# Attention and a feed-forward block in one kernel: other costs and delays in its planner, and the order that follows from them

## The chip, the cores and the metric

The kernel runs on one core of a Trainium2 chip. The metric is the device time of one execution in microseconds (us). The profile shows one execution: its engines are TensorE (PE, with its weight loads as PEld), VectorE (DVE), ScalarE (ACT), GpSimd (POOL) and SyncE (SP), which here only issues DMAs.

## The reference

Two parts follow each other. The first is attention in which a query sees only the keys of its own hash bucket; the second is a feed-forward block with an exact GELU.

```python
# q, k, v: (4, 8, 768, 64) float32; proj: (64, 6)
q_bits = (einsum('bhsd,dk->bhsk', q, proj) > 0)      # 6 bits
k_bits = (einsum('bhsd,dk->bhsk', k, proj) > 0)
mask = bucket(q_bits) == bucket(k_bits)               # (.., 768, 768)
scores = where(mask, q @ k.T / sqrt(64), -1e9)
attn = softmax(scores)                                # over the keys
x = (attn @ v) -> (3072 tokens, 512)                  # heads side by side
h = x @ w_in                                          # (3072, 2048)
g = 0.5 * h * (1 + erf(h / sqrt(2)))
out = g @ w_out                                       # (3072, 512)
```

## The kernel before, in words

All products with float32 accuracy are made of float16 matmuls: each operand is split into a high and a low half, and three products are summed (`TERMS`). Part of the first batch is done with float32 matmuls instead (`WHOLE`), which need more of PE and less of DVE.

The work is cut into *units*: 128 queries of one head against all 768 keys, 4 x 8 x 6 = 192 of them. A unit (`unit`, line 794) is a chain: four score matmuls on PE into one of two PSUM banks (ring `s`, lines 816 and 817), the row maximum on DVE (line 820), two one-column DVE instructions (guard, line 824, and shift, line 829), the exponential on ACT (line 832), which frees the bank, the norm on DVE (line 842), the split into high and low half (line 386 or 383 on any of three engines, line 848 on DVE), and a DMA that transposes the result for the product with the values (line 946). In the float32 units matmuls against a diagonal do the transpose (line 889) and line 937 the product.

Before a head's units can run, the head is prepared (`head`, line 525): load, maximum on DVE (line 537), a tiny "total" matmul on PE (line 494, in `head_scale`), a few one-column DVE instructions (lines 497 to 512), the split (line 386 or 383, 568 or 406), copies between partitions, the hash projection on PE (line 602), its sign on ACT and the mask rows. Each batch has a scale of its values (`v_scale`, maxima in line 748), and the weights are decoded, scaled and split in eight batches (`weight_pair`, lines 652 to 706). When a batch's scale and all weights are there, `hidden_scales` (lines 1087 to 1093) makes the scales of the feed-forward block on DVE.

The feed-forward block goes over 24 groups (12 chunks of 256 tokens, two halves of the 2048 hidden columns): hidden matmuls on PE (line 1120), an ACT copy out of PSUM (line 1130), GELU on ACT (line 1154), the split of its result (line 386 or 383, then 1168), the output matmuls (line 1192) and, after the second half, the drain on DVE (line 1213) and the store. Four PSUM banks (ring `hp`) serve all matmuls but the scores.

There are five passes over the heads: 256 queries of the first batch, its other 512, then one pass for each of the other batches.

The order of all instructions is made while the kernel is being built. Each piece of work is a `Step` with an engine (or several possible ones), a cost in us, a key, the steps that it needs and, for some, a ring whose slot it takes. `Plan.order` (line 110) runs the steps through a list scheduler on an imagined clock: whenever an engine is free, it takes, among the steps that are ready for it, the one with the smallest key plus its engine's offset. A step counts as ready for an engine a *hop* after the step that it needs has ended; a ring's slot is free when the last step that frees it has ended. Most rings give out their slots in program order; `hp` and `sign` to whoever comes first. The steps are then emitted in the order of their imagined starts, and on the chip each engine works through its own queue in that order, waiting on semaphores. Only the order is taken from the imagined clock, no time.

The keys are sums of a unit's running number `t` (0 to 191) and parameters of the table `PAR`: a head's key is `t` less its lead, its load subtracts `HQ` further, its maximum and total add `NS`; `VS0` is the key of the first batch's values and `SU` that of the set-up. The lead is `H0` to `H7` for the eight heads of the first pass, `G0` to `G7` for heads prepared anew in the second, and 6 + `HL` for the other batches. The feed-forward matmuls have keys from 1000 on, so PE takes them only when nothing of the attention is ready.

Of the kernel before, what the change touches and what calls it, by code (L numbers as in the profile page):

```python
# [19 lines left out]
P = 128  # L20
TC = 256
# [11 lines left out]
PAR = dict(  # L33
    SU=-208.01, NM_DVE=-120.92, NM_ACT=-21.45, NM_Pool=27.77, NM_SP=-123.06, NL_DVE=-286.91, NL_Pool=-152.59,
    NK_DVE=18.44, NK_ACT=149.22, NK_Pool=104.15, Z=-57.22, VS0=79.32, H0=-16.78, HL=-145.51, VS=19.55, G2=135.91,
    HQ=25.26, VQ=-257.12, in0=-297.08, out0=-226.11, in1=75.15, out1=-23.55, in2=208.31, out2=27.03, in3=-2.86,
    out3=-110.46, H1=295.79, H2=49.71, H3=-73.91, H4=30.82, H5=-111.35, H6=-305.61, H7=137.32, MEV=-105.25,
    MGE=-38.66, MSP=154.66, V0=61.1, QK0=151.51, QK1=139.57, QK2=162.2, MX0=-370.06, MX1=-267.83, MX2=36.74,
    EX0=32.1, EX1=300.62, EX2=464.34, NR0=126.59, NR1=149.21, NR2=345.77, HI0=-109.88, HI1=151.95, HI2=-108.38,
    LO0=-8.61, LO1=-97.74, LO2=-73.8, PV0=-123.13, PV1=19.87, PV2=-46.85, TR0=-116.16, TR1=246.71, TR2=162.28,  # L40
    V1=-192.5, V2=-1.2, Sin0=-172.88, Sin1=26.3, Sin2=-153.88, Sin3=140.04, Sout0=115.77, Sout1=-66.23,
    Sout2=146.63, Sout3=-97.45, Lin=-116.07, Pin=86.29, Qin=-266.79, Cin=76.33, Min=-479.07, Lout=304.56,
    Pout=-4.44, Qout=263.25, Cout=-138.23, Mout=364.95, G0=75.6, G1=-54.28, G3=101.75, G4=20.47, G5=15.54, G6=91.81,
    G7=-87.11, DUP0=339.38, DUP1=-11.03, DUP2=-81.43, LOW0=-236.86, LOW1=-108.93, LOW2=-52.33, PRJ0=3.84,
    PRJ1=29.31, PRJ2=211.23, MSK0=-134.81, MSK1=214.61, MSK2=42.29, DI_ACT=-147.41, DI_DVE=235.9, DI_Pool=21.15,
    WS_ACT=-362.67, WS_DVE=125.31, WS_Pool=315.49, WH_ACT=115.97, WH_DVE=-41.99, WH_Pool=-275.73, WL_ACT=74.46,
    WL_DVE=-184.87, WL_Pool=1.02, VH_ACT=5.16, VH_DVE=89.96, VH_Pool=-119.57, RND_ACT=-68.59, RND_DVE=20.61,
    RND_Pool=43.78, HI_ACT=54.52, HI_DVE=95.22, HI_Pool=-253.58, DG_ACT=203.58, DG_DVE=68.05, DG_Pool=-664.35,
    EV_ACT=-157.8, EV_DVE=400.19, EV_Pool=-118.56, GH_ACT=204.98, GH_DVE=104.62, GH_Pool=-464.69, NS0=-62.77,
    NS1=-38.83, NS2=-129.58,  # L50
)
# [19 lines left out]
class Plan:  # L71
# [38 lines left out]
    def order(self):  # L110
# [13 lines left out]
        events = []  # L124
# [16 lines left out]
        for t in set(free_at.values()):  # L141
            heapq.heappush(events, (t, -1, None))
        count = 0
        while events:
# [4 lines left out]
            for e in batch:  # L149
                if e is None:  # L150
                    continue
                for hold in e.frees:
                    hold["left"] -= 1
                    if not hold["left"]:
                        self.rings[hold["holder"].takes].append(hold["holder"].slot)
                for u in users.get(e, ()):
                    left[u] -= 1
                    for w in u.ways:
                        hop = self.SAME.get(w, 0.05) if w == e.engine else self.HOP[e.engine] + 0.12 * (w == "Pool")
                        at[u, w] = max(at.get((u, w), 0.0), now + hop)  # L160
                        heapq.heappush(events, (at[u, w], -1, None))
                    if not left[u]:
                        enlist(u)
            for engine, pool in ready.items():
# [18 lines left out]
                s = best  # L183
# [51 lines left out]
def tile_bucket_attention_moe(  # L235
# [252 lines left out]
    def head_scale(top, w, key, needs, n):  # L488
# [27 lines left out]
        pm = add("PE", 0.06 + 0.08 * n, total, key, needs, takes="hp")  # L516
        e = add("DVE", 0.12, exponent, key, [pm])
        free(pm, [e])
        e = add("DVE", 0.07, inverse, key, [e])
        if n > 1:  # L520
            e = add("DVE", 0.07, back, key, [e])
        return add("DVE", 0.07, scale, key, [e])

    def head(b, h, i, key, clear, cl):
# [19 lines left out]
        def add_move(dst, src, rd, rs):  # L544
            box = []

            def move():
# [6 lines left out]
            on = {  # L554
                "DVE": (0.27, PAR["NM_DVE"]), "ACT": (0.75, PAR["NM_ACT"]), "Pool": (0.9, PAR["NM_Pool"]),
                "SP": (0.45, PAR["NM_SP"]),
# [4 lines left out]
        def add_low(dst, rd, rs):  # L561
# [12 lines left out]

            on = {"DVE": (0.94, PAR["NL_DVE"]), "Pool": (2.8, PAR["NL_Pool"])}
            box.append(add(on, 0, low, key + PAR[f"LOW{cl}"], [hi], port=True))
# [32 lines left out]

        pp = add("PE", 0.45, project, key + PAR[f"PRJ{cl}"], [space, *set16], takes="hp")  # L610
        sg = add("ACT", 0.1 + 0.833e-3 * HS + 0.186, sign, key + PAR[f"PRJ{cl}"], [pp])
# [3 lines left out]
        for half in range(2):  # L615
            for k, dst in enumerate((0, 1)):
                box = []

                def mask(half=half, k=k, dst=dst, box=box):
# [181 lines left out]
    def unit(t, i, qs, cl, whole, made, place, back):  # L801
# [78 lines left out]
    def whole_turn(ex, nr, r, place, cl, t):  # L880
# [22 lines left out]
        for n, (k0, k1) in enumerate(((0, KT // 2), (KT // 2, KT))):  # L903
            step = []
            step.append(
                add("PE", 0.23 * (k1 - k0), lambda k0=k0, k1=k1, step=step: product(k0, k1, step), t + PAR[f"LO{cl}"], [dg], takes="hp")
            )
# [14 lines left out]
    def values(b, pr, ch, whole, vhl, turns, holds, key):  # L922
# [31 lines left out]
        for n, kt in enumerate(range(0, KT, 2)):  # L954
            kts = range(kt, min(kt + 2, KT))
            parts.append(
                add(
                    "PE", (0.96 if whole else 0.70) * nt / TC, lambda kts=kts: product(kts), key, [vh, vl, xt[b, ch], *turns, *parts],
                    takes=None if n else "hp",
                )  # L960
            )
# [119 lines left out]
    def hidden_scales(b):  # L1081
# [20 lines left out]
    for n, (b, ch, g) in enumerate(groups):  # L1102
# [8 lines left out]
        for fp in range(GF // 2):  # L1111
# [73 lines left out]
        for us in blocks:  # L1185
            for f in range(GF):
# [88 lines left out]
```

## Time and profile before

| | us |
|---|---|
| median of 3 runs | 929.64 (928.78 to 930.78) |
| the profiled execution | 928.35 |
| its span, first to last instruction | 926.4 |
| PE busy in the span | 857.1 |
| DVE busy | 734.4 |
| ACT busy | 607.8 |
| POOL busy | 347.1 |
| mean granted clock of PE | 0.983 |

A row of the profile names the line, the engine and the operation, what it writes and reads, how often it ran, its busy time and mean duration, and the idle time of the engine just before it with what ended that. A timeline row begins with its start and its length in us; a number in brackets at its end is the idle time of the engine before it. The granted clock of PE is 1.00 at full speed. Matmuls are pipelined: a row's length is longer than the distance to the next one.

### The profile page before, as it was taken

How to read it: one execution, taken by the hardware profiler on the slowest of the kernel's cores; microseconds unless marked ns; L12 is line 12 of the kernel's file. 1: busy time of each engine (PE TensorE's matmuls, PEld its weight loads, DVE VectorE, ACT ScalarE, POOL GpSimd, SP SyncE). 2: the span in 40 equal slices, each digit the busy share in tenths (PEclk: the TensorE clock that was granted, in tenths of full speed). 3: DMA queues.
4: the chain of work that ended last, by engine and by line, in shares of the span. 5: the costliest groups of instructions: out<-in, count | busy, mean ns of one | idle time of the engine just before them, and what ended most of it. 6: DMA issues, size and time to landing. Idle time of an engine off the chain costs nothing.

```text
span 926.4 us, 18281 instructions
## 1 busy us (share of the span) xinstructions
PE 857.1 (93%) x6857; PEld 576.7 (62%) x6857; DVE 734.4 (79%) x1734; ACT 607.8 (66%) x990; POOL 347.1 (37%) x323
## 2 busy tenths in 40 slices
PE   1578899996999999999999999999999999999998
PEld 0355667764575765666666666656666757575763
DVE  6888999999989999999999999899889961212122
ACT  4577799698877878757877777777865742222221
POOL 3444457285654354642335542454540400000000
PEclk9988999997999999999999999999999999999999
DMA  7653554538778788977686979788785760000000
GB/s 229 188 158 110 158 169 120 150 82 174 149 132 173 144 160 184 190 139 158 121 164 149 188 151 187 125 157 152 140 130 117 139 120 16 17 7 23 1 23 23
DMA packets 301848, 118.53 MB, mean 128 GB/s; under 512 B 241664, under 2 KB 290240, under 8 KB 301760
## 3 DMA queue, kind: packets, MB, share of 16 engines
q1 hardware_dynamic: 301680, 117.38, 58.9%
q8 instruction: 53, 0.87, 0.4%
q14 instruction: 35, 0.29, 0.1%
q10 hardware_dynamic: 80, 0.00, 0.0%
HBM read 44.31 MB, written 6.29 MB: 55 GB/s over the span
## 4 chain that ended last, share of the span: by engine, by line
PE 35%; DVE 23%; DMA 4%; issue 4%; ACT 3%; POOL 1%; SPq 0%; POOLq 0%; DVEq 0%; ACTq 0%
PE hp L1192 14%; PE hp L1120 14%; DVE rows L820 5%; DVE hl L848 4%; PE hp L946 3%; DMA pt<-hl 3%; DVE wraw L848 2%; DVE g L1168 2%; PE s L816 2%; PE s L817 2%; DMA pt<-wraw 1%; ACT p L832 1%; DVE rows L824 1%; DVE rows L829 1%; DVE rows L842 1%
## 5 line engine op out<-in xcount | busy, mean ns | idle before, releaser
L1120 PE MATMUL hp<-x,Win 128*128 128x256 f16 x2304 | 269.9, 274 | 0.2
L1192 PE MATMUL hp<-Wout,g 128*128 128x512 f16 x1152 | 261.5, 379 | 0.0
L1120 PEld LDWEIGHTS <-Win 128*128 128x128 f16 x2304 | 223.8, 98 | 41.1 <-issue 5.1
L1192 PEld LDWEIGHTS <-g 128*128 128x128 f16 x1152 | 110.3, 98 | 127.3 <-issue 5.8
L820 DVE TENSOR_REDUCE rows<-s 128x1 f32<-128x768 f32 x192 | 179.3, 947 | 4.3 <-PE s L817 3.6
L832 ACT ACTIVATE p<-s,rows 128x768 f32<-128x768 f32 x140 | 138.0, 986 | 45.3 <-DVE rows L829 23.7
L1130 ACT ACTIVATE h<-hp,ffs 128x512 f32<-128x512 f32 x96 | 65.6, 684 | 122.2 <-PE hp L1120 122.0
L816 PE MATMUL s<-Ak,Aq 88*128 88x384 f16 x360 | 120.9, 336 | 22.8 <-ACT p L832 12.8
L817 PE MATMUL s<-Bk,Bq 128*128 128x384 f16 x360 | 121.1, 336 | 0.0
L386 DVE TENSOR_SCALAR g<-h,ffs 128x512 f16<-128x512 f32 x30 | 15.2, 508 | 107.5 <-ACT h L1154 76.1
L946 PE MATMUL hp<-pt,vhl 128*64 128x256 f16 x1368 | 82.9, 274 | 0.0
L946 PEld LDWEIGHTS <-vhl 128*64 128x64 f16 x1368 | 71.7, 110 | 13.1 <-issue 12.4
L848 DVE SCALAR_TENSOR_TENSOR hl<-p,rows,hl 128x768 f16<-128x768 f32 x73 | 75.8, 1045 | 4.3 <-POOL hl L386 4.3
L1168 DVE SCALAR_TENSOR_TENSOR g<-h,ffs,g 128x512 f16<-128x512 f32 x96 | 75.5, 798 | 4.2 <-POOL g L386 2.0
L889 PEld LDWEIGHTS hp<-dr,p 128*128 128x128 f32 x468 | 61.3, 207 | 14.9 <-POOL dr L386 5.6
L889 PE MATMUL hp<-dr,p 128*128 128x128 f32 x468 | 66.0, 296 | 4.5 <-DVE dr L386 1.8
L832 ACT ACTIVATE wraw<-s,rows 128x768 f32<-128x768 f32 x52 | 51.3, 987 | 25.5 <-DVE rows L829 15.7
L817 PEld LDWEIGHTS <-Bq 128*128 128x128 f16 x360 | 35.8, 100 | 50.7 <-issue 33.7
L386 POOL TENSOR_SCALAR hl<-p,rows 128x768 f16<-128x768 f32 x34 | 38.2, 1122 | 57.4 <-DMA pt<-hl 34.0
L816 PEld LDWEIGHTS <-Aq 88*128 88x128 f16 x360 | 36.0, 100 | 31.5 <-issue 9.7
L386 POOL TENSOR_SCALAR raw<-raw,hs 64x768 f32<-64x768 f32 x30 | 34.5, 1151 | 43.2 <-ACT Aq L383 35.2
L1154 ACT ACTIVATE h<-h 128x2048 f32<-128x2048 f32 x24 | 45.9, 1911 | 0.4
(150 smaller groups left out, 1265.3 us busy)
## 6 DMA issues: line engine op xcount, KB each, us to landing
raw<-qk SPq DMA_DIRECT2D x26, 384.0 KB
vraw<-v SPq DMA_DIRECT2D x25, 384.0 KB
wraw<-w_in SPq DMA_DIRECT2D x16, 512.0 KB
wraw<-w_out SPq DMA_DIRECT2D x16, 512.0 KB
out<-o SPq DMA_DIRECT2D x11, 512.0 KB
rawe<-qk SPq DMA_DIRECT2D x8, 384.0 KB
vhl<-v SPq DMA_DIRECT2D x7, 384.0 KB
Ak<-Aq SPq DMA_DIRECT2D x24, 96.0 KB
```

The lines of the kernel that those rows point to most:

```text
L386: on.tensor_scalar(out=out, in0=in_, scalar1=scale, scalar2=bias, op0=ALU.mult, op1=ALU.add)
L816: nc.tensor.matmul(to, aq[kk, qs], ak[kk, n], start=True, stop=False)
L817: nc.tensor.matmul(to, bq[:, qs], bk[:, n], start=False, stop=True)
L820: nc.vector.tensor_reduce(out=nm, in_=both(sp), axis=AX.XY, op=ALU.max, negate=True)
L832: nc.scalar.activation(out=buf(ex).rearrange("p (b k) -> p b k", b=2), in_=both(sp), func=AF.Exp, scale=sc, bias=nb, accum_out=ssum,)
L848: nc.vector.scalar_tensor_tensor(out=buf(hi)[:, 1], in0=buf(ex), scalar=r, in1=buf(hi)[:, 0], op0=ALU.mult, op1=ALU.subtract,)
L889: nc.tensor.matmul(buf(step[0])[:, (k - k0) * P : (k - k0 + 1) * P], buf(ex)[:, words(k)], buf(dg), start=True, stop=True,)
L946: nc.tensor.matmul(pv[j * D : (j + 1) * D], buf(vh)[:, tv, kt, j * D : (j + 1) * D], buf(holds[j][0])[:, tp * KT + kt, :nt], start=kt == 0 ...
L1120: nc.tensor.matmul(buf(pair[0])[:, j * ch[1] : (j + 1) * ch[1]], win_hl[:, f0 // WB1, tw, pr, f0 % WB1 : f0 % WB1 + P], x[:, tx, pr, : ch[1]],
L1130: nc.scalar.activation(out=bufs["h"][0][:, 2 * fp : 2 * fp + 2, :nt], in_=buf(pair[0])[:, : 2 * nt].rearrange("p (j k) -> p j k", j=2), fu ...
L1168: nc.vector.scalar_tensor_tensor(out=gt[:, 1, s2, :nt], in0=h[:, s2, :nt], scalar=sg, in1=gt[:, 0, s2, :nt], op0=ALU.mult, op1=ALU.subtract,)
L1192: nc.tensor.matmul(buf(banks[u]).rearrange("p (c f) -> p c f", c=NWB), gt[:, tg, f, u * P : (u + 1) * P], wout_hl[:, :, tw, ft], start=ft ...
```

## The change

Three things change in the planner. Costs of steps: guard and shift 0.12 instead of 0.07 each, the one-column steps of a head's scale, the parts of `hidden_scales` (1.3 and 0.3 instead of 0.73 and 0.1), and small differences in others. Delays: a step on PE counts as ready 0.3 later after a step of another engine, and a slot of the rings `s` and `hp` counts as free 0.3 after the step that frees it. And all parameters of `PAR` have other values. No instruction is added or removed; which of several possible engines takes a step and the order of all steps can differ.

```diff
 PAR = dict(
-    SU=-208.01, NM_DVE=-120.92, NM_ACT=-21.45, NM_Pool=27.77, NM_SP=-123.06, NL_DVE=-286.91, NL_Pool=-152.59,
-    NK_DVE=18.44, NK_ACT=149.22, NK_Pool=104.15, Z=-57.22, VS0=79.32, H0=-16.78, HL=-145.51, VS=19.55, G2=135.91,
-    HQ=25.26, VQ=-257.12, in0=-297.08, out0=-226.11, in1=75.15, out1=-23.55, in2=208.31, out2=27.03, in3=-2.86,
-    out3=-110.46, H1=295.79, H2=49.71, H3=-73.91, H4=30.82, H5=-111.35, H6=-305.61, H7=137.32, MEV=-105.25,
-    MGE=-38.66, MSP=154.66, V0=61.1, QK0=151.51, QK1=139.57, QK2=162.2, MX0=-370.06, MX1=-267.83, MX2=36.74,
...
-    Pout=-4.44, Qout=263.25, Cout=-138.23, Mout=364.95, G0=75.6, G1=-54.28, G3=101.75, G4=20.47, G5=15.54, G6=91.81,
...
-    EV_ACT=-157.8, EV_DVE=400.19, EV_Pool=-118.56, GH_ACT=204.98, GH_DVE=104.62, GH_Pool=-464.69, NS0=-62.77,
-    NS1=-38.83, NS2=-129.58,
+    SU=127.76, NM_DVE=-50.82, NM_ACT=486.58, NM_Pool=117.29, NM_SP=-25.31, NL_DVE=-493.5, NL_Pool=-474.45,
+    NK_DVE=-132.31, NK_ACT=79.74, NK_Pool=2.67, Z=74.89, VS0=-124.73, H0=131.47, HL=-228.04, VS=52.58, G2=359.08,
+    HQ=64.5, VQ=-106.15, in0=-36.32, out0=-200.36, in1=412.34, out1=-144.5, in2=762.61, out2=16.51, in3=30.3,
+    out3=-34.08, H1=32.51, H2=-68.65, H3=-262.01, H4=46.37, H5=-1289.16, H6=68.06, H7=598.77, MEV=-78.33,
+    MGE=130.98, MSP=-83.19, V0=-113.07, QK0=182, QK1=1207.98, QK2=-161.45, MX0=-1510.49, MX1=-66.66, MX2=-201.44,
...
+    Pout=298.2, Qout=-12.86, Cout=-75.91, Mout=540.91, G0=142.37, G1=35.55, G3=97.47, G4=-48.49, G5=-25.19,
+    G6=-66.71, G7=-94.16, DUP0=403.4, DUP1=11.66, DUP2=13.47, LOW0=30.23, LOW1=108.73, LOW2=151.28, PRJ0=428.11,
...
+    EV_ACT=125.62, EV_DVE=280.99, EV_Pool=154.02, GH_ACT=-510.04, GH_DVE=36.73, GH_Pool=-122.29, NS0=-113.37,
+    NS1=-552.02, NS2=-36.65,
 )
@@ class Plan
     HOP = {"PE": 0.2, "DVE": 0.2, "ACT": 0.14, "Pool": 0.07, "SP": 0.03, "none": 0.0}
+    INTO = {"Pool": 0.12, "PE": 0.3}
+    LAG = 0.3
+    PSUM = ("s", "hp")
     ANY = ("hp", "sign")
@@ Plan.order
-        count = 0
+        count, serial = 0, -1
...
+                if isinstance(e, dict):
+                    self.rings[e["holder"].takes].append(e["holder"].slot)
+                    continue
                 for hold in e.frees:
                     hold["left"] -= 1
                     if not hold["left"]:
-                        self.rings[hold["holder"].takes].append(hold["holder"].slot)
+                        serial -= 1
+                        late = self.LAG if hold["holder"].takes in self.PSUM else 0.0
+                        heapq.heappush(events, (now + late, serial, hold))
...
-                        hop = self.SAME.get(w, 0.05) if w == e.engine else self.HOP[e.engine] + 0.12 * (w == "Pool")
+                        hop = self.SAME.get(w, 0.05) if w == e.engine else self.HOP[e.engine] + self.INTO.get(w, 0.0)
@@ head_scale
-        e = add("DVE", 0.12, exponent, key, [pm])
+        e = add("DVE", 0.07, exponent, key, [pm])
...
-            e = add("DVE", 0.07, back, key, [e])
-        return add("DVE", 0.07, scale, key, [e])
+            e = add("DVE", 0.12, back, key, [e])
+        return add("DVE", 0.12, scale, key, [e])
@@ head: copies on ACT 0.75 -> 0.84, low half on DVE 0.94 -> 1.04, projection 0.45 -> 0.55, masks on ACT 0.42 -> 0.53
@@ unit
-        sp = add("PE", 0.66, scores, t - PAR[f"QK{cl}"], made, takes="s")
+        sp = add("PE", 0.68, scores, t - PAR[f"QK{cl}"], made, takes="s")
         mx = add("DVE", 0.87, top, t - PAR[f"MX{cl}"], [sp])
-        sh = add("DVE", 0.07, guard, t - PAR[f"EX{cl}"], [mx])
-        sh = add("DVE", 0.07, shift, t - PAR[f"EX{cl}"], [sh])
+        sh = add("DVE", 0.12, guard, t - PAR[f"EX{cl}"], [mx])
+        sh = add("DVE", 0.12, shift, t - PAR[f"EX{cl}"], [sh])
@@ whole_turn: product 0.23 -> 0.235 a block; values: 0.96 -> 0.98 and 0.70 -> 0.71
@@ hidden_scales
-        a = add("DVE", 0.73, first, -10, [v_ready[b]] + [w_ready["in", c][0] for c in range(NSC)])
-        z = add("DVE", 0.1, second, -10, [a] + [w_ready["out", c][0] for c in range(NSC)])
+        a = add("DVE", 1.3, first, -10, [v_ready[b]] + [w_ready["in", c][0] for c in range(NSC)])
+        z = add("DVE", 0.3, second, -10, [a] + [w_ready["out", c][0] for c in range(NSC)])
@@ feed-forward: hidden 1.31 -> 1.32, output 1.3 -> 1.31
```

More of the change, by code (lines that the diff above doesn't have):

```diff
@@ L39 @@
[L39 to L42, printed above, removed]
-    Pout=-4.44, Qout=263.25, Cout=-138.23, Mout=364.95, G0=75.6, G1=-54.28, G3=101.75, G4=20.47, G5=15.54, G6=91.81,
@@ L44 @@
[L44 to L48, printed above, removed]
@@ new lines @@
+    MGE=130.98, MSP=-83.19, V0=-113.07, QK0=182, QK1=1207.98, QK2=-161.45, MX0=-1510.49, MX1=-66.66, MX2=-201.44,
+    EX0=-104.89, EX1=32.43, EX2=1563.75, NR0=-129.35, NR1=214.04, NR2=561.42, HI0=51.57, HI1=234.7, HI2=-120.07,
+    LO0=53.88, LO1=-52.24, LO2=-770.21, PV0=-210.5, PV1=-152.98, PV2=-172.78, TR0=711.1, TR1=-69.24, TR2=-32.28,
+    V1=-80.39, V2=-203.74, Sin0=-560.13, Sin1=337.59, Sin2=-35.36, Sin3=-249.7, Sout0=190.55, Sout1=-677.63,
+    Sout2=-127.59, Sout3=-83.13, Lin=-53.83, Pin=-40.5, Qin=61.29, Cin=124.79, Min=-142.07, Lout=-122.03,
@@ new lines @@
+    Pout=298.2, Qout=-12.86, Cout=-75.91, Mout=540.91, G0=142.37, G1=35.55, G3=97.47, G4=-48.49, G5=-25.19,
+    G6=-66.71, G7=-94.16, DUP0=403.4, DUP1=11.66, DUP2=13.47, LOW0=30.23, LOW1=108.73, LOW2=151.28, PRJ0=428.11,
+    PRJ1=40.69, PRJ2=-67.72, MSK0=129.07, MSK1=239.97, MSK2=-70.47, DI_ACT=-89.59, DI_DVE=148.57, DI_Pool=80.13,
+    WS_ACT=-1069.23, WS_DVE=119.31, WS_Pool=145.41, WH_ACT=-12.56, WH_DVE=-131.55, WH_Pool=-98.18, WL_ACT=-231.25,
+    WL_DVE=-69.14, WL_Pool=33.46, VH_ACT=3.52, VH_DVE=146.05, VH_Pool=-20.51, RND_ACT=-104.36, RND_DVE=1724.01,
@@ L51 @@
+    RND_Pool=946.3, HI_ACT=-244.94, HI_DVE=198.06, HI_Pool=194, DG_ACT=123.47, DG_DVE=2.42, DG_Pool=-800.22,
+    EV_ACT=125.62, EV_DVE=280.99, EV_Pool=154.02, GH_ACT=-510.04, GH_DVE=36.73, GH_Pool=-122.29, NS0=-113.37,
+    NS1=-552.02, NS2=-36.65,
 )
@@ L554, in add_move @@
             on = {
-                "DVE": (0.27, PAR["NM_DVE"]), "ACT": (0.75, PAR["NM_ACT"]), "Pool": (0.9, PAR["NM_Pool"]),
+                "DVE": (0.27, PAR["NM_DVE"]), "ACT": (0.84, PAR["NM_ACT"]), "Pool": (0.9, PAR["NM_Pool"]),
                 "SP": (0.45, PAR["NM_SP"]),
@@ L573, in low @@
                     subtract("Pool", out, x, a)
-            on = {"DVE": (0.94, PAR["NL_DVE"]), "Pool": (2.8, PAR["NL_Pool"])}
+            on = {"DVE": (1.04, PAR["NL_DVE"]), "Pool": (2.8, PAR["NL_Pool"])}
             box.append(add(on, 0, low, key + PAR[f"LOW{cl}"], [hi], port=True))
@@ L608, in sign @@
             nc.scalar.activation(out=signs_of(), in_=buf(pp)[:, :HS], func=AF.Sign, bias=off16)
-        pp = add("PE", 0.45, project, key + PAR[f"PRJ{cl}"], [space, *set16], takes="hp")
+        pp = add("PE", 0.55, project, key + PAR[f"PRJ{cl}"], [space, *set16], takes="hp")
         sg = add("ACT", 0.1 + 0.833e-3 * HS + 0.186, sign, key + PAR[f"PRJ{cl}"], [pp])
@@ L626, in head @@
                 on = {
-                    "DVE": (0.18, PAR["NK_DVE"]), "ACT": (0.42, PAR["NK_ACT"]), "Pool": (0.56, PAR["NK_Pool"])
+                    "DVE": (0.18, PAR["NK_DVE"]), "ACT": (0.53, PAR["NK_ACT"]), "Pool": (0.56, PAR["NK_Pool"])
                 }
@@ L905, in whole_turn @@
             step.append(
-                add("PE", 0.23 * (k1 - k0), lambda k0=k0, k1=k1, step=step: product(k0, k1, step), t + PAR[f"LO{cl}"], [dg], takes="hp")
+                add("PE", 0.235 * (k1 - k0), lambda k0=k0, k1=k1, step=step: product(k0, k1, step), t + PAR[f"LO{cl}"], [dg], takes="hp")
             )
@@ L957, in values @@
                 add(
-                    "PE", (0.96 if whole else 0.70) * nt / TC, lambda kts=kts: product(kts), key, [vh, vl, xt[b, ch], *turns, *parts],
+                    "PE", (0.98 if whole else 0.71) * nt / TC, lambda kts=kts: product(kts), key, [vh, vl, xt[b, ch], *turns, *parts],
                     takes=None if n else "hp",
@@ L1139, in tile_bucket_attention_moe @@
                     add(
-                        "PE", 1.31 * part, lambda j=j, hidden=hidden: hidden(j), LATE + n,
+                        "PE", 1.32 * part, lambda j=j, hidden=hidden: hidden(j), LATE + n,
                         [sa, w_ready["in", c // 2][1][c % 2], *x_parts[b, ch], *pair, *clear, *(early_steps if n == 0 else [])],
@@ L1202, in tile_bucket_attention_moe @@
                     needs += out_w if n == 0 else []
-                step = add("PE", 1.3 * part * len(us) / (nt // P), output, LATE + n + PAR["G2"], needs)
+                step = add("PE", 1.31 * part * len(us) / (nt // P), output, LATE + n + PAR["G2"], needs)
                 cur["out"].append(step)
```

## The prediction

> **What bounds the kernel now.** I read the first lines of the page, then a table of the span cut into its stages, then what TensorE (PE) waits for before and after the first feed-forward matmul, then the timelines around the one large hole.
>
> ```profile
> span 926.4 us, 18281 instructions
> PE 857.1 (93%) x6857; PEld 576.7 (62%) x6857; DVE 734.4 (79%) x1734; ACT 607.8 (66%) x990; POOL 347.1 (37%) x323
> ```
>
> PE is busy for 857.1 of 926.4 us, so 69.3 us of the span are PE idle. All matmuls are the same in both kernels; only their order changes. So the time can fall by PE idle and by the time that PE runs at a lower clock, and by nothing else. The stages, chosen by what PE can do in each:
>
> ```profile
> core 0: us, PE busy (x) PEld busy (x) DVE busy (x) ACT busy (x) POOL busy (x), PEclk, DMA share, GB/s
> 0.00:20.00 20.00, 1.92 (x18) 0.89 (x19) 13.37 (x34) 7.27 (x8) 7.85 (x17) 1.00 0.72 208
> 20.00:140.00 120.00, 94.16 (x694) 66.92 (x694) 108.49 (x286) 91.06 (x181) 58.21 (x53) 0.91 0.55 163
> 140.00:205.00 65.00, 63.93 (x590) 48.40 (x588) 62.93 (x159) 54.05 (x116) 39.01 (x33) 1.00 0.40 116
> 205.00:225.00 20.00, 12.32 (x75) 7.25 (x74) 19.80 (x45) 18.29 (x29) 11.87 (x10) 0.74 0.83 160
> 225.00:760.00 535.00, 522.21 (x4350) 345.33 (x4348) 492.02 (x1156) 395.84 (x612) 230.17 (x213) 1.00 0.78 152
> 760.00:922.50 162.50, 162.50 (x1138) 107.88 (x1136) 37.15 (x59) 41.32 (x48) 0.00 (x0) 1.00 0.05 17
> 922.50:926.40 3.90, 0.03 (x1) 0.00 (x0) 0.69 (x1) 0.00 (x0) 0.00 (x0) 1.00 0.18 67
> ```
>
> PE idle by stage is length less busy: 18.1, 25.8, 1.1, 7.7, 12.8, 0 and 3.9 us. The clock column adds 94.16 x 0.09 = 8.5 us from 20 to 140, and 12.32 x 0.26 = 3.2 us from 205 to 225. From 760 on only feed-forward work is left and PE has no idle at all: whatever the attention loses earlier only matters if PE stood still for it. What PE can do instead of standing still starts here:
>
> ```profile
> 120.00:140.00 20.00, 0.00 (x0) 0.00 (x0) 1.00 0.52 146
> 140.00:160.00 20.00, 1.47 (x12) 1.17 (x12) 1.00 0.36 103
> ```
>
> These are the windows of line 1120 (the hidden matmuls) alone: none before 140. So before 140 a PE wait has no filler behind it; after 140 a wait means that the queue's order was wrong, because filler stood behind the waiting step. What PE waits for, first from 140 on, then before:
>
> ```profile
> PE s L816 <- ACT wraw L832: 8.2, 12, 1.7
> PE hp L494 <- DVE tops L537: 5.8, 1, 5.8
> PE s L816 <- ACT p L832: 4.7, 11, 1.7
> ```
> ```profile
> PE hp L494 <- DVE tops L537: 19.5, 5, 7.3
> PE s L816 <- ACT p L832: 8.4, 7, 2.6
> ```
>
> From 140 on there are two kinds: 23 waits of a scores step for its PSUM bank, which the exponential on ScalarE (ACT) frees, 12.9 us in all (0.56 each), and one wait of a head's small "total" matmul for VectorE's (DVE's) maximum, 5.8 us. Together 18.7 of the 21.6 us idle between 140 and 760.
>
> **The change part by part.** *A, the banks.* A scores step takes a slot of ring `s`, and in the old plan that slot is back the moment the exponential ends. Now it is back 0.3 us later, and the exponential itself is planned later, since guard and shift cost 0.12 instead of 0.07 each. How these two stand in the trace:
>
> ```profile
> L829 DVE TENSOR_SCALAR rows<-rows 128x1 f32<-128x1 f32 x192 | 38.9, 205 | 1.2
> L824 DVE TENSOR_SCALAR rows<-rows,hs 128x1 f32<-128x1 f32 x192 | 38.3, 203 | 0.3
> 413.77 0.33 DVE L824 TENSOR_SCALAR rows<-rows,hs 128x1 f32<-128x1 f32 x2
> ```
>
> One takes 203 ns, two together 0.33 us, so the second starts 0.13 us after the first: 0.12 is what the engine gives up for one, and 0.07 was too little. Over 192 units the old plan left 192 x 2 x 0.05 = 19.2 us of DVE time out. The new plan thus expects the bank 0.3 + 2 x 0.05 = 0.4 us later, and puts a hidden or output step that is ready in front of the scores step. At most 23 x 0.4 = 9.2 us of the 12.9 go; the long ones don't go whole:
>
> ```profile
> 211.04 0.32 PE L816 MATMUL s<-Ak,Aq 88*128 88x384 f16 x1 [1.74 <-ACT wraw L832]
> 623.54 0.32 PE L816 MATMUL s<-Ak,Aq 88*128 88x384 f16 x1 [1.39 <-ACT wraw L832]
> 441.75 0.32 PE L816 MATMUL s<-Ak,Aq 88*128 88x384 f16 x1 [0.15 <-ACT p L832]
> ```
>
> The least is nothing, if a new order makes as many new waits as it removes. I take half, -4.6, as the plan's times drift from the chip's by more than 0.4 us in places (these rows), so waits will arise anew.
>
> *B, the hole at 212 to 218.* The head's total waits for the maximum of line 537:
>
> ```profile
> 207.88 1.30 DVE L1087 TENSOR_SCALAR ffs<-inv,inv_v 128x4 f32<-128x4 f32 x1
> 209.68 0.20 DVE L829 TENSOR_SCALAR rows<-rows 128x1 f32<-128x1 f32 x1
> 209.79 0.40 DVE L1093 TENSOR_SCALAR ffs<-inv,ffs 128x4 f32<-128x4 f32 x1
> 217.08 0.94 DVE L537 TENSOR_REDUCE tops<-raw 128x1 bf16<-128x768 f32 x1
> ```
> ```profile
> 218.07 0.19 PE L494 MATMUL hp<-tops,twin 128*128 128x1 bf16 x2 [5.77 <-DVE tops L537]
> 220.84 4.33 PE L1120 MATMUL hp<-x,Win 128*128 128x256 f16 x23
> 810.56 10.48 PE hp L1120 x96
> ```
>
> Ahead of that maximum in DVE's queue stand the hidden scales of the new batch: 207.88 to 209.68 is 1.8 us, planned at 0.73, now at 1.3; the second part is 0.40, planned at 0.1, now at 0.3. The corrections make 0.77 us here, and about eight guard-and-shift pairs of the 20 us before it another 0.8: some 1.6 of the 5.8 us. The new order thus need not have this hole, but nothing makes it impossible. Its whole price is 5.8 us and the clock behind it, 3.2 us by the stage table: 23 hidden matmuls took 4.33 us there, 188 ns each, against 10.48 / 96 = 109 ns late in the run. That is 9.0 us. I take half, -4.5; the ends are -9.0 and, if one more such hole arises, +9.0.
> The page "TensorE: Matmul & The Clock Gate" of the Trainium skill, Part 1, says that an idle window of about 3.4 us halves the clock and that one busy window of about 3.4 us restores it. By that rule such a hole costs only 1.7 us of clock, B as a whole 7.5, and the forecast would be 0.75 us higher; the trace's 3.2 decides. That short waits cost no clock agrees with the trace: granted clock 1.00 from 225 to 760, with 12.8 us of idle in it.
>
> *C, steps into PE.* Every result now counts for PE 0.3 us later. That isn't a recorded duration: the maximum above ends at 217.08 + 0.94 = 218.02 and the total starts at 218.07. It is a margin. From 140 on it costs nothing: if the chain of a unit got later by 0.3 at each of two PE steps, 192 units on two banks, one after another, would be 192 x 0.6 / 2 = 58 us late at the most, and the 162.5 us of pure feed-forward work behind 760 cover that. Without that cover it would be those 58 us. The longer matmul costs (0.66 to 0.68, 0.70 to 0.71, 1.31 to 1.32) and those of the small moves change no instruction: nothing by themselves.
>
> *D, the start.* No filler hides anything here, so order counts directly. By the keys of the table (smallest first, `rawe` and `wraw` handed out in program order) the first loads before are pass 1's head 6 at 40 - 91.81 - 25.26 = -77, head 0 at 16.78 - 25.26 = -8, head 1 right behind, and `v` at 79. The trace has that order:
>
> ```profile
> 1.39 0.81 SPq L534 DMA_DIRECT2D raw<-qk  x1
> 2.26 0.89 SPq L534 DMA_DIRECT2D rawe<-qk  x2
> 3.19 1.77 SPq L743 DMA_DIRECT2D wraw<-v  x3
> 23.82 0.48 PE L816 MATMUL s<-Ak,Aq 88*128 88x384 f16 x1 [0.47 <-POOL Ak L386]
> ```
> ```profile
> raw<-qk SPq DMA_DIRECT2D x26, 384.0 KB
> ```
>
> After it, head 0 has -131.47 - 64.5 = -196, `v` -125, head 1 2 - 32.51 - 64.5 = -95, pass 1's head 6 40 + 66.71 - 64.5 = 42. So head 0 moves ahead of one load, and head 1 moves behind three of 384 KB. At the 208 GB/s of the first 20 us one such load is 1.9 us (393 KB / 208 GB/s), three are 5.7. The set-up on DVE (key -208, now 128), on which every head's total waits, moves behind the maxima of `v`. The ends are -1.9 (head 0 sooner) and +5.7 (head 1 later, and nothing makes it up). I take +1.5: head 0's two units give PE its first work, the later heads queue behind DVE, which is busy for 108.49 of the next 120 us anyway.
>
> Sum: -4.6 - 4.5 + 1.5 = -7.6; 926.4 - 7.6 = 918.8 us of span. The profiled execution took 928.35, 1.95 around its span, and the median of the runs is 929.64, 1.29 above that execution. So 918.8 + 1.95 + 1.29 = 922.0.
>
> **The rivals.**
> *Blocked totals (slower).* The queue of PE is in order, and a head's total stands in it wherever the plan expected DVE to be. The last three batches have 24 heads, each with such a total. In the new table DVE does a head's maximum later: its key is the unit's time plus 185 (-6 + 228.04 - 36.65) instead of plus 10 (-6 + 145.51 - 129.58). If the hole at 218 stays in some place and one more arises, it is A -4.6, B +9.0, D +1.5: +5.9, 932.3 of span, 935.5. It decides once waits of line 494 after 140, with the clock behind them, pass about 9.0 + 3.1 = 12 us. For it: the corrected costs explain 1.6 of 5.8 us. Against: of these totals one alone has a wait of note in the list above, and the new plan starts them with 0.3 us to spare.
> *The start eats it (no change).* `v` ahead of the heads costs all 5.7 us, and the set-up behind three maxima, at 0.94 each like the one of line 537, another 2.8: +8.5 against -9.1 of A and B, 925.8 of span, 929.0. It would show as first scores at about 32 instead of 23.82. For it: no filler before 140. Against: DVE is idle for 6.6 of the first 20 us, room for the set-up's small steps.
> *All of it (faster still).* A -9.2, B -9.0, D -1.9: -20.1, 906.3 of span, 909.5. Against it: no order avoids every wait.
> That the plan's costs do not come nearer to the chip is no rival for guard and shift (0.13 us) or the hidden scales, by the rows above; for the 0.3 into PE it is so, and C prices that at nothing.
>
> **How the numbers follow.** Forecast 0.54, blocked totals 0.24, the start 0.14, all of it 0.08. A measurement of this kernel can tell about 0.2%, 1.9 us, from no change. Faster is 0.54 + 0.08 = 0.62, the same 0.14, slower 0.24. The forecast's own range goes from A and B at three quarters (-13.6 + 1.5 = -12.1, so 917.5) to a quarter (-4.5 + 1.5 = -3.0, 926.6). The whole range runs from 910, where nearly all of A, B and D is had, to 937, just past one more hole; about 0.12 of the slower case and 0.05 of the fastest lie outside.
>
> **What would show it.** Right: PE waits for `s` after 140 near 8 us instead of 12.9, no wait of line 494 above 3 us after 140, granted clock 1.00 in every window after 140, PE idle from 140 to 760 near 14 us instead of 21.6, and first scores within 3 us of 23.82. Wrong: a wait of line 494 of 5 us or more after 140 (blocked totals); a first scores matmul near 32, or more than 50 us of PE idle before 140 against 43.9 (the start); the `s` waits unchanged, which would say that 0.4 us in the plan moves nothing.

## The result, and the profile after

| | before | after |
|---|---|---|
| median, us (4 runs each) | 929.86 (928.78 to 930.78) | 922.16 (920.94 to 922.72) |
| profiled execution, us | 928.35 | 922.43 |
| span, us | 926.4 | 920.3 |
| mean granted clock of PE | 0.983 | 0.983 |

The ratio is 0.9916 [0.9899, 0.9933], so 0.84% faster. The forecast was 922.0. The sum came out; most of its terms did not, as the sections below show.

The first lines of the page of the changed kernel (all its lines stand 8 higher than before: 824 for the scores' 816, 502 for the total's 494, 1128 for the hidden matmuls' 1120):

```profile
span 920.3 us, 18292 instructions
PE 852.7 (93%) x6857; PEld 577.0 (63%) x6857; DVE 732.2 (80%) x1717; ACT 615.6 (67%) x997; POOL 376.1 (41%) x356
```

PE is busy 4.4 us less for the same 6857 matmuls at the same mean clock, and idle 67.6 instead of 69.3 us. The stages, at nearly the cuts used for before:

```profile
core 0: us, PE busy (x) PEld busy (x) DVE busy (x) ACT busy (x) POOL busy (x), PEclk, DMA share, GB/s
0.00:20.00 20.00, 2.10 (x17) 0.96 (x18) 13.31 (x37) 6.43 (x8) 7.15 (x17) 1.00 0.78 222
20.00:140.00 120.00, 95.36 (x731) 67.58 (x730) 111.37 (x275) 96.81 (x190) 69.05 (x62) 0.91 0.53 158
140.00:205.00 65.00, 60.65 (x562) 47.39 (x562) 61.48 (x157) 52.29 (x108) 38.47 (x34) 1.00 0.43 121
205.00:225.00 20.00, 18.03 (x139) 13.02 (x140) 19.25 (x42) 19.45 (x33) 12.54 (x14) 0.91 0.67 133
225.00:760.00 535.00, 520.10 (x4317) 344.49 (x4316) 488.44 (x1147) 397.15 (x611) 248.87 (x233) 0.99 0.76 150
760.00:916.40 156.40, 156.40 (x1096) 103.55 (x1094) 37.68 (x62) 43.52 (x51) 0.00 (x0) 1.00 0.08 20
```

PE's idle from 140 to 760 is 4.35 + 1.97 + 14.9 = 21.2 us, against 21.6 before. The stretch from 205 to 225 is much better, the one ahead of it and the long one behind it are worse. What PE waits for from 140 on, then before 140:

```profile
PE s L824 <- ACT p L840: 5.0, 6, 2.7
PE hp L945 <- DVE tiny L372: 2.7, 1, 2.7
PE hp L502 <- DVE x L981: 2.7, 2, 1.4
PE s L824 <- ACT wraw L840: 2.5, 6, 0.7
PE hp L1128 <- DVE o L1221: 2.3, 2, 1.3
PE hp L954 <- DMA pt<-wraw: 1.7, 2, 0.9
...
PE hp L502 <- DVE tops L545: 0.2, 1, 0.2
```
```profile
PE hp L502 <- DVE tops L545: 10.3, 6, 3.7
PE hp L502 <- DVE tops L466: 8.3, 1, 8.3
PE s L824 <- ACT p L840: 4.7, 3, 3.0
```

The waits for score banks after 140 fall from 12.9 to 7.5 us and the total's wait from 5.8 to 0.2. Waits that were not in the list before take their place: a product step of the float32 units for a DVE instruction (2.7), totals for a DVE copy of line 981 (2.7), hidden matmuls for the drain (2.3), products for a transposing DMA (1.7).

Where the time went, in a measure that idle time alone does not give: each matmul is taken at the distance from start to start that it has in undisturbed stretches (hidden 109 ns, output 216, scores 165, products 57.7 and 124, the others 55 to 118), and the *loss* of a stretch is its length less the sum of these. So a low clock and short pauses between matmuls count too.

| loss of PE, us | 0-140 | 140-225 | 225-360 | 360-460 | 460-760 | 760-end | all |
|---|---|---|---|---|---|---|---|
| before | 62.3 | 12.0 | 6.7 | 5.3 | 13.0 | 4.1 | 103.5 |
| after | 58.1 | 7.6 | 7.2 | 11.7 | 8.5 | 4.3 | 97.4 |

The difference, 6.1 us, is that of the spans. The gain comes from the start (4.2), from the stretch with the hole (4.4) and from 460 to 760 (4.5); between 360 and 460 the changed kernel gives 6.4 us back. In that stretch PE's idle rises from 2.2 to 6.5 us and the granted clock falls from 1.00 to 0.97.

### The profile page after: what moved, and what is told of

Read it like the earlier page. It is cut to its first block, busy times and chain, and to the rows that moved or that the text cites. A ratio compares the mean times of both kernels' runs of the same rounds, so it can differ in the third digit from the quotient of the medians.

```text
span 920.3 us, 18292 instructions
## 1 busy us (share of the span) xinstructions
PE 852.7 (93%) x6857; PEld 577.0 (63%) x6857; DVE 732.2 (80%) x1717; ACT 615.6 (67%) x997; POOL 376.1 (41%) x356
## 5 line engine op out<-in xcount | busy, mean ns | idle before, releaser
L840 ACT ACTIVATE p<-s,rows 128x768 f32<-128x768 f32 x140 | 138.1, 987 | 62.3 <-DVE rows L837 40.3
L856 DVE SCALAR_TENSOR_TENSOR hl<-p,rows,hl 128x768 f16<-128x768 f32 x73 | 78.6, 1078 | 2.9 <-POOL hl L394 1.5
L394 POOL TENSOR_SCALAR raw<-raw,hs 64x768 f32<-64x768 f32 x41 | 45.1, 1100 | 23.9 <-ACT Aq L391 20.6
L394 POOL TENSOR_SCALAR g<-h,ffs 128x512 f16<-128x512 f32 x39 | 34.3, 885 | 40.7 <-ACT h L1162 30.8
```

The source lines that it names most:

```text
L394: on.tensor_scalar(out=out, in0=in_, scalar1=scale, scalar2=bias, op0=ALU.mult, op1=ALU.add)
L840: nc.scalar.activation(out=buf(ex).rearrange("p (b k) -> p b k", b=2), in_=both(sp), func=AF.Exp, scale=sc, bias=nb, accum_out=ssum,)
L856: nc.vector.scalar_tensor_tensor(out=buf(hi)[:, 1], in0=buf(ex), scalar=r, in1=buf(hi)[:, 0], op0=ALU.mult, op1=ALU.subtract,)
```

## The experiments

Each ratio is to the kernel before, measured in the same session; its medians there were 929.73 to 930.56, so times of different sessions, such as 922.16, can be compared to about 1 us.

Three theories stood against each other, T1, T2 and T3 where they need a name. T1 is the prediction's: better costs and delays remove single waits, each with a price. T2: the new keys bring the gain. T3: keys and plan only fit each other; an order made with part of the change is simply another order, and its time is that of the whole order.

**Half of the change each.** e1 is the changed kernel with the keys of before, e2 the kernel before with the new keys.

```diff
 e1, against the changed kernel:
 PAR = dict(
-    SU=127.76, NM_DVE=-50.82, NM_ACT=486.58, NM_Pool=117.29,
+    SU=-208.01, NM_DVE=-120.92, NM_ACT=-21.45, NM_Pool=27.77,
...
 e2, against the kernel before: these lines the other way round
```

> The planner with all new costs and delays, with the old parameters. If the costs and delays themselves make the better order, this is faster than before by 3 us or more (927 or less) and its waits for a score bank after 140 fall from 12.9 us to about 8. If the gain sits in the parameters, it stays within 2 us of 929.9. If parameters and planner only fit each other, it is slower than before, 933 or more.

> The old costs and delays with the new parameters. If the costs and delays make the better order: about 930, with score-bank waits of about 13 us after 140. If the gain sits in the parameters (the start, above all): 922 to 925, with the first GELU as early as in the changed kernel (203). If the two only fit each other: 933 or more.

e1: 962.05 us, ratio to before 1.0322 [1.0266, 1.0377]; e2: 961.20, 1.0319 [1.0272, 1.0365]. Each half alone costs over 3%. T1 and T2 both fail. The two runs show that these keys need this plan. They do not show that the gain needs the plan: whether other values, chosen for the unchanged planner, would reach 922 as well was not tried.

**The new keys with part of the new plan.** e3 leaves out both delays, e4 keeps the delays and takes the costs of before, e9 leaves out the 0.3 us into PE, e10 the 0.3 us on PSUM banks.

```diff
 e3:
-    INTO = {"Pool": 0.12, "PE": 0.3}
-    LAG = 0.3
+    INTO = {"Pool": 0.12}
+    LAG = 0.0
 e4:
-        sh = add("DVE", 0.12, guard, t - PAR[f"EX{cl}"], [mx])
+        sh = add("DVE", 0.07, guard, t - PAR[f"EX{cl}"], [mx])
...
 e9: the line INTO alone
 e10: the line LAG alone
```

> The changed kernel without the two delays (0.3 into TensorE, 0.3 for a PSUM slot); costs and parameters new. If the delays remove the score-bank waits: those go back from 7.5 us to about 12 after 140, and the time is 3 to 5 us above 922. If the delays only move waits to other places: within 2 us of 922, with the sum of TensorE's waits after 140 unchanged at about 20.

> The changed kernel with the old costs; delays and parameters new. If the costs of guard, shift and the hidden scales matter as the prediction had it: the hole at the first GELU is back near 6 us and the time is 3 to 5 us above 922. If they don't: within 2 us of 922.

> The changed kernel with the 0.3 us into a PE step taken out of the plan; its costs, the 0.3 us on PSUM banks and all keys stay. The prediction's own pricing (its part C: the margin costs nothing and brings nothing): 922, within 2 us. Rival, that the keys fit one plan only (the run without either delay gave 946.9): 930 or more, PE waits of scores after 140 above 11 us instead of 7.5. If the bank delay of 0.3 us is the one that matters, this run stays near 922 and the next, without that one, goes near 947.

> The changed kernel with the 0.3 us on PSUM banks taken out of the plan; all else stays. The prediction's part A (the bank delay by itself is three quarters of 0.4 us per wait): the scores' waits after 140 go back to about 11 to 13 us from 7.5, and the time to 922.2 + 4.6 x 0.75 = 925.6. Rival, that the keys fit one plan only: 930 or more, with less PE work done between 225 and 760 and not only more waits of scores.

e3: 946.91, 1.0168 [1.0121, 1.0215]. e4: 935.36, 1.0050 [1.0025, 1.0075]. e9: 946.38, 1.0161 [1.0121, 1.0201]. e10: 949.72, 1.0199 [1.0150, 1.0247]. All four are slower than before, and 13 to 28 us slower than the changed kernel. A margin that the prediction priced at nothing (C, taken away in e9) moves 24 us, and the bank delay, priced at 3.5 in e10's expectation, moves 28. The signs named in the expectations: the waits for score banks from 140 on are 20.3 us in e3, 13.5 in e4, 20.5 in e9 and 16.2 in e10, against 7.5 in the changed kernel. In e4, with the old costs, the hole of nearly 6 us at the first GELU is not back: the longest PE wait between 192 and 208 us (GELU at 195.69) is 1.6 us. So an order without the hole does not need the new costs. From the 51st (e3, e4, e9) and the 95th matmul (e10) on, these four have another order than the changed kernel. T3 stands.

**One edit in the order, nothing else.** e5 takes the finished order of before and moves the total that stands in the hole at 212 (and what depends on it) behind the next two scores steps. e6 moves, in the same order, each of the 36 scores steps whose bank was planned to come free less than 0.4 us earlier behind the feed-forward step that follows it: part A by hand.

```diff
 e5, ahead of the emission:
+    totals = [s for s in steps if s.emit.__name__ == "total"]
+    first = steps.index(totals[15])
+    scores = [n for n in range(first, len(steps)) if steps[n].emit.__name__ == "scores"][:2]
+    late, kept = [steps[first]], []
+    for s in steps[first + 1 : scores[-1] + 1]:
+        (late if any(n in late for n in s.needs) else kept).append(s)
+    steps[first : scores[-1] + 1] = kept + late
 e6:
+            if before and a.start - freed_by[before].end < 0.4 and z.key >= 1000 and a not in z.needs:
+                moved.append((a, z))
```

> The order before, unchanged but for one head total: the one that waited 5.77 us at 218 stands behind the next two score steps instead of ahead of them. If it blocked work that was ready (the prediction's B): the hole and the slow clock behind it go, 5 to 9 us faster, 921 to 925. If nothing was ready there, since ScalarE ran GELU with two table loads and held both score banks: the score step waits in its place, over 4 us, and the time is within 1.5 us of 929.9.

> The order before, but 36 score steps, planned less than 0.4 us after their bank came free, each change places with the feed-forward step right behind them. If this alone is the gain of a later bank (the prediction's A): the waits for a score bank after 140 fall from 12.9 to 6 us or less and the time by 4 to 9 us, to 921 to 926. If such waits only move (VectorE gets its scores later, other steps wait): within 2 us of 929.9, with the sum of TensorE's waits after 140 not lower.

e5: 931.48, 1.0007 [0.9973, 1.0042]: no gain. The hole has another last waiter and is as long (PE's timeline of e5), and a second wait for a score bank, 3.82 us until 226.48, follows it:

```profile
215.03 0.48 PE L816 MATMUL s<-Ak,Aq 88*128 88x384 f16 x1 [5.99 <-ACT p L832]
218.08 4.59 PE L1120 MATMUL hp<-x,Win 128*128 128x256 f16 x36 [0.26 <-DVE hs L497]
```

Moving the total thus does not remove the hole; the reason lies on ACT and DVE. Their timelines in the kernel before:

```profile
212.64 1.28 ACT L1154 ACT_TABLE_LOAD   x1
213.93 1.91 ACT L1154 ACTIVATE h<-h 128x2048 f32<-128x2048 f32 x1
215.86 1.28 ACT L832 ACT_TABLE_LOAD   x1
217.16 0.99 ACT L832 ACTIVATE p<-s,rows 128x768 f32<-128x768 f32 x1
```
```profile
215.16 0.20 DVE L829 TENSOR_SCALAR rows<-rows 128x1 f32<-128x1 f32 x1
219.83 0.74 DVE L1168 SCALAR_TENSOR_TENSOR g<-h,ffs,g 128x512 f16<-128x512 f32 x1
```

From 212.64 to 217.16 ACT holds GELU and the table loads on both sides of it, 4.5 us, and no exponential runs, so both score banks stay taken. But the next exponential needs a shift (line 829) that DVE ends only at 215.16 + 0.20 = 215.36; with ACT free it could have started there instead of at 217.16. By these rows GELU and its loads hold the bank for the last 1.8 us of the hole; before that it is the order of work on DVE. And there is no filler: this is the first group of the feed-forward, and the code lets a hidden step of the second group start only behind the first group's split, which ends at 219.83 + 0.74 = 220.57; the next hidden matmul of the prediction's timeline starts at 220.84. The changed kernel has the same three ACT instructions, at 203.09, and the same gap in the hidden matmuls (200.7 to 211.2, before 208.1 to 220.8); in that gap lie float32 products that were still to do:

```profile
202.76 1.46 PE L945 MATMUL hp<-pt,vhl 128*64 128x256 f32 x10
206.97 2.82 PE L945 MATMUL hp<-pt,vhl 128*64 128x256 f32 x10 [2.75 <-DVE tiny L372]
```

As the two timelines read, the hole is shorter not because a blocked step gave way to filler, but because attention work was left to lie in it. No run changes this alone.

e6: 944.73, 1.0128 [1.0077, 1.0178], 15 us slower. PE's waits from 140 on in e6:

```profile
PE s L816 <- ACT wraw L832: 9.1, 13, 1.9
PE s L816 <- ACT p L832: 9.0, 19, 1.6
PE hp L494 <- DVE tops L537: 5.8, 1, 5.8
```

Neither expectation came: the waits for banks are 18.1 us instead of 12.9. Each swap puts a step planned at 1.3 us in front of a scores step, where the 23 waits for a bank were 0.56 us each on average. That this delays the unit's maximum and so the next exponentials is a reading, not a measurement; the last scores do start at 759 instead of 743. A saving of 0.4 us per wait, added up over the waits, is not what the queue gives.

**How near is the next order?** e7 and e8 move every value of the table at random by up to 1 (the same moves), in the kernel before and in the changed one; e11 does it with other moves in the changed one. (The table's values lie between -1510 and 1724.)

```diff
 e11:
-    SU=127.76, NM_DVE=-50.82, NM_ACT=486.58, NM_Pool=117.29,
+    SU=128.67, NM_DVE=-49.92, NM_ACT=485.69, NM_Pool=116.46,
...
```

> The kernel before, with every parameter moved by a random number between -1 and 1. If the order is robust: within 3 us of 929.9. If a set of parameters is a narrow optimum of its planner, as the two exchanged halves (961 and 962) suggest: 5 to 35 us slower.

> The changed kernel, with every parameter moved by a random number between -1 and 1. If the order is robust: within 3 us of 922. If it is a narrow optimum: 5 to 35 us slower.

> The changed kernel with every key moved at random by up to 1, by another seed than before. If the changed order is a narrow hit, this is again slow: 930 or more, PE busy from 225 to 760 below 515. If the first seed's 944.4 was one unlucky exchange, this stays within 922 to 926. The kernel before stayed at 929.4 under its random move.

e7: 929.38, 0.9989 [0.9961, 1.0017]; e8: 944.42, 1.0146 [1.0099, 1.0193]; e11: 923.66, 0.9926 [0.9890, 0.9962]. I had first read e7 against e8 as a robust kernel before and a narrow changed one. That reading falls: e7's instructions stand in the same order as those of before on every engine, so it is the same program measured again, and e11's differ from those of the changed kernel by one DVE instruction that changes places with another. In e8 the order is the same for the first 1,160 of PE's 6857 matmuls and another one from there on. So the time belongs to the order: where the keys' shift leaves the order, the time stays; where the order changes from a point on, as in e8, it was 22 us worse.

**The start alone.** e12 has the new plan, the new keys of the set-up, the weights and the first two passes, and the old keys of the other passes. The offsets of the engines (such as `NM_DVE`), which act in all passes, are the old ones too.

```diff
 e12, against the changed kernel:
-    NM_DVE=-50.82, HL=-228.04, G2=359.08, QK2=-161.45, MX2=-201.44, EX2=1563.75,
+    NM_DVE=-120.92, HL=-145.51, G2=135.91, QK2=162.2, MX2=36.74, EX2=464.34,
...
     SU=127.76, H0=131.47, HQ=64.5, VQ=-106.15, G0=142.37, QK0=182, QK1=1207.98,
```

> The new plan with the new keys of the start (weights, set-up, the first two passes) and the old keys of the later passes. With all keys old the new plan gave 962.05. If the start alone gains what the trace of the changed kernel shows before 140 (4 us of PE work): PE work by 140 as in the changed kernel (busy near 95.4 from 20 to 140, first scores near 22.9) and 958 in all, since the later passes stay as bad. If the later keys don't matter and the start sets the rest: below 935. The prediction's part D (the new start loses 1.5): 963.5.

e12: 957.41, 1.0276 [1.0220, 1.0332]. Its loss up to 140 is 57.0 us, e1's 68.4, that of the changed kernel 58.1: under the new plan the better start belongs to the start's keys. Under the old plan the same keys lose 67.5 (e2, below), so here too keys and plan go together. Of the 11.4 us between e1 and e12 only 4.6 are left in the total (957.41 against 962.05).

**Where the other orders lose.** The traces side by side, with the loss as above, the start of batch 0's last output matmul (the 288th of 1152) and that of batch 1's first hidden matmul (the 577th of 2304):

| order | us | batch 0's last output | batch 1's first hidden | 0-140 | 140-360 | 360-460 | 460-760 |
|---|---|---|---|---|---|---|---|
| after | 922.16 | 423.5 | 398.6 | 58.1 | 14.8 | 11.7 | 8.5 |
| before | 929.86 | 429.9 | 399.8 | 62.3 | 18.7 | 5.3 | 13.0 |
| e4 | 935.36 | 414.5 | 414.7 | 60.4 | 24.4 | 16.3 | 7.2 |
| e8 | 944.42 | 405.5 | 419.8 | 59.2 | 23.7 | 25.1 | 8.0 |
| e6 | 944.73 | 438.8 | 407.7 | 63.4 | 25.3 | 6.4 | 20.3 |
| e9 | 946.38 | 399.9 | 421.1 | 63.7 | 16.3 | 25.2 | 11.1 |
| e3 | 946.91 | 408.1 | 423.5 | 60.4 | 25.1 | 21.6 | 9.7 |
| e10 | 949.72 | 418.0 | 418.9 | 68.8 | 22.6 | 13.7 | 16.3 |
| e12 | 957.41 | 410.8 | 428.5 | 57.0 | 29.2 | 24.8 | 16.8 |
| e2 | 961.20 | 407.1 | 422.1 | 67.5 | 18.2 | 24.5 | 22.8 |
| e1 | 962.05 | 403.4 | 432.1 | 68.4 | 16.0 | 29.9 | 19.3 |

(e5, e7 and e11 are left out: their loss from 360 to 460 is 5.1, 5.3 and 11.0 like that of the kernel they come from.) In all eight orders that were planned anew, batch 1's feed-forward begins 16 to 34 us later than in the changed kernel, and all eight lose more than it between 360 and 460: six of them 10 to 18 us more (e1, e2, e3, e8, e9, e12), e4 4.6 and e10 2.0. The two columns of starts fit this: in the changed kernel, in that before and in e6 batch 0's feed-forward still has work for 25 to 31 us after batch 1's has begun. In the same six orders it ends 14 to 29 us before batch 1's begins, and nothing of the feed-forward lies between; in e4 and e10 the two meet within 1 us. The rest of their loss lies in other places, in no stage common to all. What happens there, in e9 against the changed kernel: windows of the hidden matmuls alone (busy time of PE and of its weight loads with counts, clock, DMA share, GB/s), first of the changed kernel, then of e9; behind them the window of all engines and PE's timeline, both of e9.

```profile
380.00:400.00 20.00, 1.37 (x13) 1.34 (x14) 0.91 0.78 171
400.00:420.00 20.00, 9.93 (x85) 7.97 (x83) 1.00 0.77 159
```
```profile
380.00:400.00 20.00, 0.00 (x0) 0.00 (x0) 1.00 0.63 126
400.00:420.00 20.00, 0.00 (x0) 0.00 (x0) 0.66 0.66 148
420.00:440.00 20.00, 11.12 (x96) 9.29 (x96) 1.00 0.91 145
```
```profile
400.00:420.00 20.00, 10.83 (x65) 5.90 (x64) 17.58 (x42) 10.28 (x19) 7.26 (x7) 0.66 0.66 148
```
```profile
399.69 0.60 PE L1200 MATMUL hp<-Wout,g 128*128 128x512 f16 x2
...
401.44 0.19 PE L502 MATMUL hp<-tops,twin 128*128 128x1 bf16 x2
406.90 0.48 PE L824 MATMUL s<-Ak,Aq 88*128 88x384 f16 x1 [5.26 <-ACT p L840]
407.17 0.52 PE L825 MATMUL s<-Bk,Bq 128*128 128x384 f16 x1
407.49 0.52 PE L824 MATMUL s<-Ak,Aq 88*128 88x384 f16 x1
...
412.21 0.48 PE L824 MATMUL s<-Ak,Aq 88*128 88x384 f16 x1 [2.55 <-ACT p L840]
...
415.00 0.48 PE L824 MATMUL s<-Ak,Aq 88*128 88x384 f16 x1 [1.35 <-ACT p L840]
...
416.37 3.58 PE L954 MATMUL hp<-pt,vhl 128*64 128x256 f16 x36
419.88 0.34 PE L824 MATMUL s<-Ak,Aq 88*128 88x384 f16 x1
```

Batch 0's feed-forward is used up: its last output matmul runs at 399.69. Batch 1's hidden matmuls need the outputs of all eight heads, and its attention is not through (scores of its last unit at 409.1; 386.2 before, 396.5 in the changed kernel). From 400 to 420 PE has the attention alone, and the attention goes at the pace of DVE (busy 17.58 of 20; ACT only 10.28): PE works 10.83 of 20 us, at a clock of 0.66. From 360 to 460 e9 loses 13.5 us more than the changed kernel, of the 23.1 by which its span is longer. This is read from the traces side by side; an order with more of batch 0's feed-forward kept for this stretch was not tried.

## Why the prediction was right, step by step

**The premise** ("the time can fall by PE idle and by the time that PE runs at a lower clock, and by nothing else") was too narrow. Idle fell by 1.7 us, the mean clock stayed at 0.983, busy fell by 4.4. Busy time holds short pauses and ends that are modelled. The Trainium skill, "Perfetto Trace Analysis", § Identifying the Most-Contended Engine, says that the busy share of the matmuls is a poor measure of how close PE is to its limit, because they are pipelined; the 852.7 and 857.1 us for the same matmuls agree.

**"After 140 a wait means that the queue's order was wrong, because filler stood behind the waiting step"** was wrong at the first group (e5's hole), where no filler was ready by the data. In e9 and the five orders like it the same holds at the border of batches 0 and 1.

**A** forecast -4.6 through the waits for banks, "near 8 us instead of 12.9". They became 7.5. But e11, with the same order on PE and 1.5 us more time, has 13.3 us of them, so this sign says little by itself. From 460 to 760 the forecast held: these waits go from 6.0 to 2.1 us (3.3 in e11) and the loss falls by 4.5. From 360 to 460 they rise from 1.6 to 3.4 and the loss grows by 6.4. So 225 to 760 is 2.3 us worse in loss (25.0 to 27.3, before rounding), and PE's idle from 140 to 760 is 21.2, not "near 14". What failed is the step from "the waits fall" to "the time falls by as much": the sum has no term for what a new order loses in other places, here at the border of batches 0 and 1. e6 showed that a similar edit by hand costs 15 us, and e10 that the bank delay cannot be priced apart from the rest of the order.

**B** forecast -4.5 for the hole; the stretch from 140 to 225 gained 4.4 (12.0 to 7.6), 1.6 of it by clock (18.03 x 0.09 = 1.6 us of clock lost at 205 to 225 instead of 3.2). No wait of a total is above 3 us after 140 (2.9 us in all, the longest 1.4), as said; the clock of 1.00 in every window after 140 did not come. The size was right, the cause was not: moving the total gains nothing (e5), and the old costs do not bring the hole back (e4). Both score banks were taken, because the next exponential waited for DVE until 215.36 and then for GELU and its loads until 217.16, while the second group was not ready.

**C** held as far as it can be seen: the last scores start 10.6 us later (753.3 against 742.7), under a feed-forward tail of 156.4 us, and nothing shows of it at the end. But e9 showed that the margin is no free extra: the order without it takes 946.38.

**D** forecast +1.5 and was wrong in sign: -4.2 us of loss by 140, with first scores at 22.90 instead of 23.82. The order of the loads came as the keys said (SP's queue, changed kernel):

```profile
1.40 0.81 SPq L542 DMA_DIRECT2D rawe<-qk  x1
2.26 1.59 SPq L751 DMA_DIRECT2D wraw<-v  x3
3.89 2.31 SPq L542 DMA_DIRECT2D rawe<-qk  x1
```

Head 1's load is issued right behind the three of `v`, at 3.89. DVE's maximum of head 1 and PE's wait for it in the changed kernel; behind them head 1's maximum and the longest wait of a total in the kernel before:

```profile
11.23 0.95 DVE L545 TENSOR_REDUCE tops<-rawe 128x1 bf16<-128x768 f32 x1
12.23 0.19 PE L502 MATMUL hp<-tops,twin 128*128 128x1 bf16 x2 [3.75 <-DVE tops L545]
```
```profile
8.69 0.95 DVE L537 TENSOR_REDUCE tops<-rawe 128x1 bf16<-128x768 f32 x1 [1.67 <-DMA rawe<-qk]
17.32 0.19 PE L494 MATMUL hp<-tops,twin 128*128 128x1 bf16 x2 [7.33 <-DVE tops L537]
```

Head 1's maximum starts 2.5 us later, and the set-up's total runs at 8.26 instead of 3.29, as the prediction said. The scores start 0.9 us earlier all the same, and before 140 the totals wait 20.2 us in all (10.3 + 8.3 + 1.6) against 22.8 (19.5 + 3.3). The step that failed put the loads' time and the set-up on the path to the first scores without a row that showed that path. Of the 4.2 us idle time gives 1.4 (42.5 against 43.9); which pauses make up the rest is open.

So -4.6 - 4.5 + 1.5 = -7.6 met a fall of 6.1 in span and 7.7 in the median, as -4.2 (start), -4.4 (hole), +2.3 (225 to 760) and +0.2. The right total is in part luck: two errors of 5.7 (D) and 6.9 us (A, if 225 to 760 is booked on it) went against each other. The span came out 1.5 us above its forecast (920.3 against 918.8). The median fits because the profiled execution lies 0.3 us above its median, where that of the kernel before lay 1.5 below.

**The rivals.** A hole behind a total did not come up in the changed kernel (2.9 us of such waits after 140). In e8 it did: totals wait 9.3 us there from 140 on, and the granted clock is 0.83 at 205 to 225. The rival that was not named is the one that six of the eight newly planned orders show: an order that runs out of filler at the border of two batches. All eight are slower than before, by 0.5 to 3.2%.

What stays open: why the changed order, alone among those planned with new keys, brings batch 1's attention through in time, and whether filler kept back would beat it. No run shows how the values of either table were found. If they were picked as the best of many orders tried, slower neighbours are what one would expect.

## What to carry to other kernels

When a planner makes the order, a corrected cost or a margin has no price of its own: the order changes from the first exchange on, and it is the whole order that is timed, so plan several neighbours and time them before reading a gain as that of the correction. Before calling a wait a fault of the queue's order, look up by the data what could have run in its place; here nothing could at the first group and, in six orders, between two batches. Keeping filler for such stretches is worth trying; it was not tried here. Before taking a variant for a test of robustness, see whether its order differs at all.

## What the runs showed of the hardware

The price of a long wait depends on what follows it. In e9, after the 5.26 us wait, scores run at half pace (406.90, 407.17, 407.49: 0.27 and 0.32 us apart instead of 0.165) for the next 9 us, as they come in bursts of 2.8 us and less with waits of 1.35 to 2.55 between; at 419.88, behind a run of 36 products without a pause (from 416.37, 98 ns each instead of 57.7), they are at full pace again. The Trainium skill, "TensorE: Matmul & The Clock Gate", Part 1, says that full clock comes back after about 3.4 us of sustained work; e9's trace agrees, as bursts of up to 2.8 us did not bring it back and a run of 3.6 us did. The hole of 5.8 us in the kernel before was followed by scores and hidden matmuls without a pause; there the granted clock was 0.50 for another 6.1 us (218.07 to 224.20), and it cost 3.2 us.

Shorter waits cost clock too. In the changed kernel a wait of 2.73 us until 386.14 is followed by a granted clock of 0.50 from 387.4 to 390.8, and waits of 1.33 and 1.01 us close together, until 427.79, by the same from 428.4 to 431.8, though PE is busy through both stretches.

A GELU between exponentials held ACT for 1.28 + 1.91 + 1.28 = 4.5 us, and no exponential freed one of the two score banks meanwhile. In the hole of the kernel before only the last 1.8 us were due to it, as DVE had not finished the shift before 215.36.
